# Constants built on VectorE instead of with iotas on GpSimd, and keys and values of a batch projected side by side in 512 columns

## The chip, the cores and the metric

One core of one Trainium2 chip. The metric is the device time of one execution in microseconds (us), median of several executions. A profile of one execution goes with each kernel; its span is about 2 us shorter than the execution's time. Times inside a profile are counted from the start of its span. "Granted clock" is the share of TensorE's full clock that an execution was given, by its record. TensorE, VectorE (DVE), ScalarE (ACT), GpSimd (POOL) and SyncE (SP) are the engines; PEld is TensorE's loading of weights.

## The reference

Attention with projected keys and values, then a gated feed-forward. Cut to what matters:

```python
# q, k, v: 8 batches, 8 heads, 1024 rows, 64 wide; E, F: 64 x 1024
k_proj = np.einsum('ks,bhsd->bhkd', E, k)
v_proj = np.einsum('ks,bhsd->bhkd', F, v)
scores = (1 / 8) * np.matmul(q, k_proj.transpose(0, 1, 3, 2))   # 1024 x 64 a head
attn = exp(scores - max) / (sum + 1e-09)
x = np.matmul(attn, v_proj)                       # heads put side by side: 8192 x 512
out = (sigmoid(x @ w_gate) * (x @ w_val)) @ w_out # 512 -> 1536 -> 512
```

All inputs and the output are float32; the kernel casts to bf16 on loading.

## The kernel before: the parts that matter

The kernel records operations with what they read and write; a wait is made of each dependence. The loads of k, q, v and the weights cast, and are all issued by GpSimd, in this order. E and F come through SyncE.

```python
load_k(0)
pool(lambda e: e.iota(col_i[:, :], [[1, P]], channel_multiplier=0), w=["col_i"])
pool(lambda e: e.iota(row_i[:, :], [[1, 1]], channel_multiplier=1), w=["row_i"])
load_q_half(0, 0)
load_v(0)
# ... three more iotas for patterns ...
load_w(0)          # w_gate and w_val, first piece (256 of 1536 columns)
load_w(1)
load_q_half(0, 1)
load_w(2)
load_w(3)
```

VectorE makes an identity of the counted columns and rows, and selectors for the softmax's sums:

```python
dve(lambda e: e.tensor_copy(col_f[:, :], col_i[:, :]), ["col_i"], ["col_f"])
dve(lambda e: e.tensor_copy(row_f[:, :], row_i[:, :]), ["row_i"], ["row_f"])
for t, n in ((identf, "identf"), (ident, "ident")):
    dve(lambda e, t=t: e.tensor_scalar(t[:, :], col_f[:, :], row_f[:, 0:1], None, op0=ALU.is_equal), ...)
# ... half, low_i, low_f, negm, dsel8, bsel8, bsel, dsel ...
```

TensorE begins with the first half batch. It cannot do a thing before the identity:

```python
start_loads()
constants()
project_consts()          # E and F turned with identf: 8 transposes, then EFT on ScalarE
busy(56)                  # 56 dummy 128x128 matmuls, to warm the clock
bk = whole.next()
project(0, 0, [bk, bk], 0)    # k, needs EFT and the k load
keep_k(bk, 0)
turn_k(whole)
qt, sc, den, bc, xo = half_unit(0, whole)
qt(0); qt(1)              # q transposes, need the first q half
sc(0); sc(1)              # scores and exp
den()                     # sums, reciprocal
bks = [whole.next(), whole.next()]
project(1, 1, bks, 0)     # v, needs the v load
keep_v(bks, 0, ["ACT", "DVE", "ACT", "DVE"])
busy(8); bc(0); busy(4); xo(0); bc(1); xo(1); busy(10)
# then the feed-forward of batch b, with the attention of batch b+1 in between
```

From the third batch on (six batches), keys and values are projected together in the middle of the feed-forward, in 32 matmuls of 256 columns, and the keys are turned by a DMA transpose:

```python
def kv():
    bk = att.next()
    project(2 * b % 3, 0, [bk, bk], 0)           # keys: 16 matmuls of 256 columns
    project((2 * b + 1) % 3, 1, [bk, bk], 256)   # values: 16 more
    # ... b == 1 differs ...
    act(kpd[:, :, :, :], bank[bk][:, 0:256] ... .to_broadcast([P, NR, 2, DH]), ...)  # 128 x 512
    keep_v([bk, bk], 256, ["ACT"] * 4)           # four copies, 64 x 256 each
```

The softmax here doesn't subtract the row's maximum and nothing guards it: scores larger than these inputs give would overflow.

Of the kernel before, what the change touches and what calls it, by code (L numbers as in the profile page):

```python
# [7 lines left out]
ALU = mybir.AluOpType  # L8
# [110 lines left out]
def bass_linformer_attn__then__ffn_glu_sigmoid_kernel(  # L119
# [18 lines left out]
    with contextlib.ExitStack() as es:  # L138
# [5 lines left out]
        col_i = sbuf("col_i", [P, P], I32)  # L144
        row_i = sbuf("row_i", [P, 1], I32)
        pat_i = sbuf("pat_i", [P, P], I32)
        pat4_i = sbuf("pat4_i", [P, 64], I32)
        eight_i = sbuf("eight_i", [P, 8], I32)
        low_i = sbuf("low_i", [P, 3], I32)
        col_f = sbuf("col_f", [P, P], FP32)  # L150
        row_f = sbuf("row_f", [P, 1], FP32)
        pat_f = sbuf("pat_f", [P, P], FP32)
        pat4_f = sbuf("pat4_f", [P, 64], FP32)
        eight_f = sbuf("eight_f", [P, 8], FP32)
        low_f = sbuf("low_f", [P, 2], FP32)
        half = sbuf("half", [P, 2], FP32)
        negm = sbuf("negm", [P, 1], FP32)
# [13 lines left out]
        kpd = sbuf("kpd", [P, NR, 2, DH], BF16)  # L171
# [114 lines left out]
        def start_loads():  # L286
            for src, rows, n in ((E, slice(0, 64), "E"), (F, slice(64, 128), "F")):
                add(
                    "SP",
                    lambda e, src=src, rows=rows: e.dma_start(EF[rows, :], src[:, :]),  # L290
                    w=[("EF", n)],
                    dma="in" + n,
                )
            load_k(0)
            pool(lambda e: e.iota(col_i[:, :], [[1, P]], channel_multiplier=0), w=["col_i"])
            pool(lambda e: e.iota(row_i[:, :], [[1, 1]], channel_multiplier=1), w=["row_i"])
            load_q_half(0, 0)
            load_v(0)
            pool(
                lambda e: e.iota(  # L300
                    pat_i[:, :], [[-2, 4], [0, 4], [1, 8]], channel_multiplier=0
                ),
                w=["pat_i"],
            )
            pool(lambda e: e.iota(eight_i[:, :], [[1, 8]], channel_multiplier=0), w=["eight_i"])
            pool(
                lambda e: e.iota(
                    pat4_i[:, :], [[-2, 2], [0, 8], [1, 4]], channel_multiplier=0
                ),
                w=["pat4_i"],  # L310
            )
            load_w(0)
            load_w(1)
            load_q_half(0, 1)
            load_w(2)
            load_w(3)

        def constants():
            dve(lambda e: e.tensor_copy(col_f[:, :], col_i[:, :]), ["col_i"], ["col_f"])
            dve(lambda e: e.tensor_copy(row_f[:, :], row_i[:, :]), ["row_i"], ["row_f"])  # L320
            for t, n in ((identf, "identf"), (ident, "ident")):
                dve(
                    lambda e, t=t: e.tensor_scalar(  # L323
                        t[:, :], col_f[:, :], row_f[:, 0:1], None, op0=ALU.is_equal
                    ),
                    ["col_f", "row_f"],
                    [n],
                )
            for n, op in ((0, ALU.is_ge), (1, ALU.is_lt)):
                dve(  # L330
                    lambda e, n=n, op=op: e.tensor_scalar(  # L331
                        half[:, n : n + 1], row_f[:, :], 64.0, None, op0=op
                    ),
                    ["row_f"],
                    [("half", n)],
                )
            for n, bit in ((0, 7), (1, 8), (2, 3)):
                dve(
                    lambda e, n=n, bit=bit: e.tensor_single_scalar(
                        low_i[:, n : n + 1], row_i[:, :], bit, op=ALU.bitwise_and  # L340
                    ),
                    ["row_i"],
                    [("low", n)],
                )
            for n in range(2):
                dve(
                    lambda e, n=n: e.tensor_copy(low_f[:, n : n + 1], low_i[:, 2 * n : 2 * n + 1]),
                    [("low", 2 * n)],
                    [("low_f", n)],
                )  # L350
            dve(
                lambda e: e.tensor_scalar(negm[:, :], low_i[:, 1:2], -0.125, None, op0=ALU.mult),
                [("low", 1)],
                ["negm"],
            )
            dve(lambda e: e.tensor_copy(pat_f[:, :], pat_i[:, :]), ["pat_i"], ["pat_f"])
            dve(lambda e: e.tensor_copy(eight_f[:, :], eight_i[:, :]), ["eight_i"], ["eight_f"])
            for n in range(2):
                dve(
                    lambda e, n=n: e.tensor_scalar(  # L360
                        dsel8[:, n, :, :].rearrange("p a c -> p (a c)"),
                        pat_f[:, :],
                        half[:, n : n + 1],
                        None,
                        op0=ALU.is_equal,
                    ),
                    ["pat_f", ("half", n)],
                    [("dsel8", n)],
                )
            dve(  # L370
                lambda e: e.tensor_scalar(
                    bsel8[:, :, :, :].rearrange("p c h d -> p (c h) d"),
                    eight_f[:, :].unsqueeze(2).to_broadcast([P, 8, 64]),
                    low_f[:, 0:1],
                    0.5,
                    op0=ALU.is_equal,
                    op1=ALU.mult,
                ),
                ["eight_f", ("low_f", 0)],
                ["bsel8"],  # L380
            )
            dve(
                lambda e: e.tensor_scalar(
                    bsel[:, :, :, :].rearrange("p c h d -> p (c h) d"),
                    eight_f[:, 0:4].unsqueeze(2).to_broadcast([P, 4, 64]),
                    low_f[:, 1:2],
                    0.25,
                    op0=ALU.is_equal,
                    op1=ALU.mult,
                ),  # L390
                ["eight_f", ("low_f", 1)],
                ["bsel"],
            )
            dve(lambda e: e.tensor_copy(pat4_f[:, :], pat4_i[:, :]), ["pat4_i"], ["pat4_f"])
            for n in range(2):
                dve(
                    lambda e, n=n: e.tensor_scalar(
                        dsel[:, n, :, :].rearrange("p a c -> p (a c)"),
                        pat4_f[:, :],
                        half[:, n : n + 1],  # L400
                        None,
                        op0=ALU.is_equal,
                    ),
                    ["pat4_f", ("half", n)],
                    [("dsel", n)],
                )
# [79 lines left out]
        def half_unit(hf, ring):  # L486
# [51 lines left out]
            def den():  # L538
                bk = ring.next()
                for n in range(4):  # L540
                    for c in range(4):
# [21 lines left out]
                        rhl[:, 0:P], rhi[:, 0:P], negm[:, 0:1], rden[:, 0:P], ALU.mult, ALU.add  # L563
                    ),
                    [("rden", 0), "rhi", "negm"],
# [67 lines left out]
        def attention(b):  # L633
            s = b % 2

            def kv():
                bk = att.next()
                project(2 * b % 3, 0, [bk, bk], 0)
                project((2 * b + 1) % 3, 1, [bk, bk], 256)
                if b == 1:  # L640
                    keep_k(bk, 0)
                    keep_v([bk, bk], 256, ["ACT"] * 4)
                    return
                act(
                    kpd[:, :, :, :],
                    bank[bk][:, 0:256]
                    .rearrange("p (r d) -> p r d", r=NR)
                    .unsqueeze(2)
                    .to_broadcast([P, NR, 2, DH]),
                    [],  # L650
                    ["kpd"],
                    b=bk,
                )
                keep_v([bk, bk], 256, ["ACT"] * 4)

            def turn_kd():
                if b == 1:
# [5 lines left out]
                        kpD[:, :, :].rearrange("p (r h) c -> p r (h c)", h=2),  # L663
                        kpd[:, :, :, :].rearrange("p r g d -> p (r g d)"),
# [56 lines left out]
            def split():  # L721
                rd = [("rden", c) for c in range(4)]
                dve(lambda e: e.tensor_copy(rhi[:, :], rden[:, :]), rd, ["rhi"])  # L723
                dve(
                    lambda e: e.scalar_tensor_tensor(  # L725
                        rhl[:, :], rhi[:, :], negm[:, 0:1], rden[:, :], ALU.mult, ALU.add
                    ),
                    rd + ["rhi", "negm"],
                    ["rhl"],
                )  # L730
# [189 lines left out]
        load(wO[:, :, :], moe_w_out.rearrange("(m p) c -> p m c", p=P), ["wO"], "wO")  # L920

# [85 lines left out]
```

## Time and profile before

| | before |
|---|---|
| time, median of 4 executions | 580.79 us |
| span of the profile | 577.98 us |
| TensorE's first matmul | 15.48 |
| projection of k, of v (first half batch) | 21.21, 27.59 |
| first feed-forward matmul at full pace | 33.46 |
| from there to the end | 544.5 |
| one projection of keys and values, third batch on, in the chain | 1.87 |

The last column of a timeline line, in brackets, is how long the engine had been idle before it and what ended that. A line of the chain gives its start, its length, and what was at work. The lines themselves are in the prediction below.

### The profile page before, as it was taken

What the parts mean: (1) busy time and instruction counts of PE and PEld (TensorE: products, weight loads), DVE (VectorE), ACT (ScalarE), POOL (GpSimd) and SP (SyncE); (2) the same over time, 40 slices, a digit from 0 to 9 for tenths busy, and PEclk for the clock granted to TensorE, in tenths of its full rate; (3) what the DMA queues carried; (4) which work ended last, traced back from release to release, by engine and by line L of the source; (5) the groups of instructions that cost most, each with busy time, mean ns of one, the idle gap of its engine ahead of it and who ended that gap; (6) DMA issues with size and microseconds to landing.
All of it is one profiled execution on the core that took longest, in us unless ns stands there. A gap on an engine that the chain in (4) does not pass through costs nothing.

```text
span 578.0 us, 7834 instructions
## 1 busy us (share of the span) xinstructions
PE 555.5 (96%) x3110; PEld 252.1 (44%) x3110; DVE 246.4 (43%) x381; ACT 175.1 (30%) x317; POOL 101.5 (18%) x139
## 2 busy tenths in 40 slices
PE   0899999999999999999999999999999999999997
PEld 0644434544444444444444444444445444444443
DVE  0446355335443356235363354433562353633332
ACT  0355443352223422333223522234223332222220
POOL 1800010102600053000810026000520008000000
PEclk9999999999999999999999999999999999999999
DMA  6999979892576047650696125771311011100002
GB/s 109 160 203 200 186 125 194 150 195 58 108 148 119 37 65 134 127 90 36 111 173 104 44 57 108 148 119 37 75 56 45 21 38 38 37 36 19 36 37 91
DMA packets 74212, 56.01 MB, mean 97 GB/s; under 512 B 34528, under 2 KB 65760, under 8 KB 74176
## 3 DMA queue, kind: packets, MB, share of 16 engines
q0 software_dynamic: 31776, 29.89, 33.7%
q1 hardware_dynamic: 42400, 25.63, 17.5%
q8 instruction: 24, 0.39, 0.3%
q14 instruction: 12, 0.10, 0.1%
HBM read 60.29 MB, written 16.78 MB: 133 GB/s over the span
## 4 chain that ended last, share of the span: by engine, by line
PE 94%; issue 2%; DVE 2%; ACT 1%; POOL 0%; POOLq 0%; DVEq 0%
PE pF L218 85%; PE pA L218 9%; DVE rden L715 1%; ACT eT L222 0%; DVE xT L606 0%; ACT qT L222 0%; POOL KV L236 0%; DVE rden L553 0%; DVE vpD L464 0%; DVE identf L323 0%; DVE rhl L725 0%; DVE ost L878 0%; DVE hT L851 0%; DVE rhi L723 0%; ACT kp L222 0%
## 5 line engine op out<-in xcount | busy, mean ns | idle before, releaser
L851 DVE SCALAR_TENSOR_TENSOR hT<-sig,pF 128x512 bf16<-128x512 f32 x192 | 130.9, 685 | 203.3 <-PE pF L218 155.8
L222 ACT ACTIVATE sig<-pF 128x512 f32<-128x512 f32 x192 | 114.8, 599 | 315.9 <-PE pF L218 312.9
L218 PE MATMUL pF<-xT,wG 128*128 128x512 bf16 x768 | 198.6, 380 | 0.6 <-ACT rb L222 0.3
L218 PE MATMUL pF<-xT,wV 128*128 128x512 bf16 x768 | 198.2, 379 | 0.2 <-DVE xT L606 0.2
L218 PE MATMUL pF<-wO,hT 128*128 128x512 bf16 x720 | 165.4, 380 | 0.0
L218 PEld LDWEIGHTS pF<-xT,wV 128*128 128x128 bf16 x768 | 75.1, 98 | 90.9 <-issue 0.6
L218 PEld LDWEIGHTS pF<-xT,wG 128*128 128x128 bf16 x768 | 72.1, 98 | 94.2 <-issue 11.8
L760 POOL PARTITION_BROADCAST rb<-rrow x96 | 70.8, 798 | 219.3 <-DMA rrow<-rden 213.9
L218 PEld LDWEIGHTS pF<-wO,hT 128*128 128x128 bf16 x720 | 69.1, 98 | 87.3 <-issue 5.8
L878 DVE TENSOR_SCALAR ost<-pF 128x512 f32<-128x512 f32 x60 | 41.5, 691 | 94.0 <-PE pF L218 94.0
L222 ACT ACTIVATE eT<-pA 128x512 bf16<-128x512 f32 x63 | 32.7, 603 | 10.2 <-PE pA L218 10.2
L785 DVE TENSOR_TENSOR xT<-pA,rb 128x512 bf16<-128x512 f32 x56 | 34.7, 681 | 0.0
L715 DVE RECIPROCAL rden<-pA 128x128 f32<-128x128 f32 x28 | 23.7, 909 | 0.0
L236 POOL DMA_DIRECT2D KV<-in_k_dram x8 | 7.5, 937 | 82.4 <-PE pF L218 80.4
L236 POOL DMA_DIRECT2D KV<-in_v_dram x8 | 7.2, 895 | 75.0 <-PE pA L218 75.0
L218 PE MATMUL pA<-identf,EF 128*128 128x128 f32 x8 | 1.9, 421 | 15.5 <-DVE half L331 15.5
L218 PE MATMUL pA<-KV,EFT 128*64 128x256 bf16 x240 | 14.6, 274 | 0.0
L218 PEld LDWEIGHTS pA<-KV,EFT 128*64 128x64 bf16 x240 | 12.5, 110 | 3.1 <-issue 3.0
L222 ACT ACTIVATE kpd<-pA 128x512 bf16<-128x512 f32 x6 | 3.6, 597 | 28.4 <-PE pA L218 28.4
L218 PE MATMUL pA<-eT,vpD 64*64 64x512 bf16 (+1 forms) x136 | 10.4, 370 | 0.3 <-DVE vpD L464 0.3
L218 PE MATMUL pA<-qT,kpD 64*64 64x512 bf16 (+1 forms) x140 | 10.4, 367 | 0.3 <-ACT qT L222 0.3
L222 ACT ACTIVATE vpD<-pA 64x256 bf16<-64x256 f32 x28 | 10.5, 375 | 0.5
(74 smaller groups left out, 109.1 us busy)
## 6 DMA issues: line engine op xcount, KB each, us to landing
out_dram<-ost SPq DMA_DIRECT2D x64, 256.0 KB, 2.0
KV<-in_k_dram POOLq DMA_DIRECT2D x8, 1024.0 KB, 10.7
KV<-in_v_dram POOLq DMA_DIRECT2D x8, 1024.0 KB, 11.3
Qb<-in_q_dram POOLq DMA_DIRECT2D x7, 1024.0 KB, 15.2
wO<-in_moe_w_out_dram POOLq DMA_DIRECT2D x1, 1536.0 KB, 44.5
Qb<-in_q_dram POOLq DMA_DIRECT2D x2, 512.0 KB, 10.3
wG<-in_moe_w_gate_dram POOLq DMA_DIRECT2D x2, 512.0 KB, 18.3
wV<-in_moe_w_val_dram POOLq DMA_DIRECT2D x2, 512.0 KB, 20.1
```

Source lines behind the costliest of these rows:

```text
L218: return add("PE", lambda e: e.matmul(o, lhsT, rhs, **kw), r=r, x=[("bank", b)])
L222: return add("ACT", lambda e: e.activation(o, i, func, scale=scale), r=r, w=w, x=x)
L236: add("POOL", lambda e: e.dma_start(o, i), r=r, w=w, dma=sem)
L715: lambda e, cc=cc: e.reciprocal(rden[:, cc], bank[bk][:, cc]),
L760: lambda e, n=n, i=2 * rnd + c, j=j, parts=parts: e.partition_broadcast(rb[0:parts, n, :], rrow[32 * j : 32 * j + 1, i, :], channels=parts),
L785: lambda e, r=r, g=g, n=n, bk=bks[g]: e.tensor_tensor(xT[s][:, r, :, 256 * g : 256 * g + 256], bank[bk][:, :].rearrange("p (f c) -> p f c" ...
L851: lambda e: e.scalar_tensor_tensor(hT[blk % 2][:, m, :], sg[:, :], 1.0, bank[pv][:, :], ALU.add, ALU.mult,),
L878: lambda e: e.tensor_scalar(o[:, :], bank[pb][:, :], 0.5, None, op0=ALU.mult),
```

## The change

Its intent: no iota, so that GpSimd needs no library of code before the loads of q and v and before the identity; and half as many matmuls in the six later projections. The row and column counters are made on VectorE by doubling a counted row, and a 32x32-block transpose of it; GpSimd only writes 0, 32, 64 and 96 into the four quarters of a column. The library for the broadcasts (first needed for the third batch) is loaded by an instruction of its own after the first batches' loads.

```diff
+            for i in range(4):
+                pool(lambda e, i=i: e.memset(quad[32 * i : 32 * i + 32, :], 32.0 * i), w=[("quad", i)])
             load_k(0)
-            pool(lambda e: e.iota(col_i[:, :], [[1, P]], channel_multiplier=0), w=["col_i"])
-            pool(lambda e: e.iota(row_i[:, :], [[1, 1]], channel_multiplier=1), w=["row_i"])
             load_q_half(0, 0)
             load_v(0)
-            (three more iotas)
...
+            dve(lambda e: e.memset(count[:, 0:1], 0.0), [], ["count"])
+            for i in range(7):
+                n = 1 << i
+                dve(... e.tensor_scalar(count[:, n : 2 * n], count[:, 0:n], float(n), None, op0=ALU.add) ...)
+            (four patterns, one transpose, row_f = rows + quad)
...                                   # the identity and the selectors from these
+                for t in range(NT):
+                    for w in range(2):            # keys, then values, of step t
+                        n = (2 * b + w) % 3
+                        src = KV[n][:, :, :].rearrange("p h (t d) -> p t h d", t=NT)
+                        mm(bk, bank[bk][64 * w : 64 * w + 64, :], EFT[:, t, 64 * w : 64 * w + 64],
+                           src[:, t, :, :], ..., tp=(0, 64 * w))       # 512 columns
-                act(kpd ...)                      # 128 x 512
-                keep_v([bk, bk], 256, ["ACT"] * 4)
+                act(kpd ...)                      # 64 x 1024
+                for g in range(2):
+                    act(vpD[64 * g : 64 * g + 64, :, :] ..., bank[bk][64:128, :], ...)   # 64 x 512
...
-                        kpD[:, :, :].rearrange("p (r h) c -> p r (h c)", h=2),
-                        kpd[:, :, :, :].rearrange("p r g d -> p (r g d)"),
+                        kpD[:, :, :],
+                        kpd[:, :, :, :].rearrange("p h g d -> p (h g d)"),
...
+        pool(lambda e: e.load_library(spread_library))    # after the load of w_out
```

## The prediction

> **What bounds the kernel now.** I read the page's busy shares and the chain that ended last first, then the timeline of the first 35 us, then the DMA view, then the chain again around one projection. All times below are us from the span's start unless said otherwise.
>
> ```profile
> PE 555.5 (96%) x3110; PEld 252.1 (44%) x3110; DVE 246.4 (43%) x381; ACT 175.1 (30%) x317; POOL 101.5 (18%) x139
> ...
> PE   0899999999999999999999999999999999999997
> ...
> PE 94%; issue 2%; DVE 2%; ACT 1%; POOL 0%; POOLq 0%; DVEq 0%
> ```
>
> TensorE is busy in every slice but the first, and 94% of the chain is its own work. Whatever moves no TensorE time and no start of TensorE is worth nothing. The first slice is empty, and the timeline says why:
>
> ```profile
> 1.24 1.01 POOL L236 DMA_DIRECT2D KV<-in_k_dram  x1 [0.80 <-POOLq L992]
> 1.38 0.57 SPq L290 DMA_DIRECT2D EF<-in_F_dram  x1
> 13.96 0.23 POOL L295 IOTA col_i<- 128x128 int32 x1 [11.71 <-issue]
> ...
> 14.24 1.07 POOL L236 DMA_DIRECT2D Qb<-in_q_dram  x1
> 14.55 0.78 DVE L323 TENSOR_SCALAR identf<-col_f,row_f 128x128 f32<-128x128 f32 x1
> 15.48 1.94 PE L218 MATMUL pA<-identf,EF 128*128 128x128 f32 x8 [15.48 <-DVE half L331]
> 17.22 4.07 PE L218 MATMUL pF<-ident 128*128 128x128 bf16 x56
> 21.21 1.06 PE L218 MATMUL pA<-KV,EFT 128*64 128x256 bf16 x16
> 27.59 1.06 PE L218 MATMUL pF<-KV,EFT 128*64 128x256 bf16 x16
> ```
>
> GpSimd sits 11.71 before the first iota, behind a library load that the instruction order shows there and the trace gives no busy time. Everything hangs on it: the identity for TensorE (first matmul at 15.48), and, because GpSimd issues in order, the loads of q and v at 14.24 and 15.33. The DMA view of the first 20 us gives the landings:
>
> ```profile
> KV<-in_k_dram POOLq DMA_DIRECT2D x1, 1024.0 KB, 11.1
> KV<-in_v_dram POOLq DMA_DIRECT2D x1, 1024.0 KB, 10.6
> ...
> EF<-in_F_dram SPq DMA_DIRECT2D x1, 256.0 KB, 4.2
> ```
>
> So k lands at 1.24+11.1=12.3, F at 1.38+4.2=5.6, v at 15.33+10.6=25.9. The DMA engines stand idle from about 12.3 to 16.
>
> The chain around one of the six steady projections, which the second part of the change rewrites:
>
> ```profile
> 160.55 12.19 PE pF L218 x56
> 172.74 1.87 PE pA L218 x32
> 174.61 13.06 PE pF L218 x60
> 187.66 0.56 PE pA L218 x8
> ```
>
> **What the Trainium skill says.** "GPSIMD Engine Reference", section 2.1 Instruction dispatch: the first call to a freshly loaded kernel pays about 6 us for fetching it, with no visible profile instruction. The trace agrees that nothing is visible, but the gap is 11.71, and I use that. "TensorEngine Tiling (Array Packing)", section Tiling Modes and its Key Properties: with 128 rows and 64 columns there are two tiles, and different tiles run in parallel. The trace agrees: 32 projection matmuls of 273 ns each take 1.87, not 8.7. They already run in pairs, 117 ns a pair of 256 columns. "DMA: Bandwidth & Descriptors", section Queues, rings and completion order: an engine takes turns between queues, a packet at a time. The trace agrees: the transpose of the keys lands in 2.4 in the last batch, with no loads in flight, and 9.4 in the median.
>
> **The change, part 1: constants.** Removed: five iotas and their library load on GpSimd. Added: four memsets ahead of the k load (memsets at the span's start follow each other by 0.03, so the k load goes out about 0.2 later), and a chain on VectorE: one memset, seven adds, each waiting for the last, four pattern copies, one 128x128 transpose, one add, then the identity. The small VectorE instructions at 14.23 to 15.8 follow each other by 0.1 to 0.2; estimate: 13 by 0.15, plus 0.4 for the transpose and 0.5 for the identity, is 2.9, from about 0.8, so done near 3.7. F lands at 5.6. So the identity is no longer the last to arrive; E and F are. TensorE starts near 5.6 instead of 15.48, almost 10 sooner. This is not the gain, since the next thing it needs is data.
>
> Follow TensorE in the new order. Transposes of E and F 5.6 to 7.5 (1.94). The 56 warming matmuls, 3.9 by the chain, to 11.4. Keys: the load lands at 12.3+0.2=12.5; TensorE waits 1.1. The k projection and what follows to the q transposes took 21.28 to 23.19 in the chain, 1.9: so 14.4. The q half now queues directly behind k instead of 2 us after an idle queue. Rate: between v's landing (25.9) and the landing of the next batch's q (issued 23.72, 26.3 to landing: 50.0) 4608 KB landed in 24.1, that is 191 KB per us, the queue full. So the q half (512 KB) lands 2.7 after k, at 15.2, and v (1024 KB) 5.4 later, at 20.6. The q transposes start at 15.2 (before 23.1); from there to the v projection took 4.4 (23.19 to 27.59), so TensorE is ready at 19.6 and waits for v until 20.6. Before, v had landed at 25.9 and was used at 27.59. So the v projection moves by 27.6-20.6=7.0. The rest, to the first full feed-forward matmuls at 33.46, is arithmetic: the denominator's reciprocal is now done while v is awaited, which takes the two VectorE copies of v (0.44 each) forward, but the warming matmuls (0.6 and 0.4) and the copies of rb on ScalarE stay in the way; I give 0.3 for it. Gain of part 1: about 7.2.
>
> Is it kept? The DMA queue gains only 25.9-20.6=5.3, so each later load has up to 1.9 less slack. Slack before, from issue plus landing in the trace: second piece of w (needed 36.8, landed 31 to 32) 5; third w_val piece (needed 42.5, landed 39.9) 2.6; next v (issued 25.46, landed 36.6 later, at 62.1, needed 65.9) 3.8; w_out (landed 26.33+44.5=70.8, needed 74.8) 4.0. All stay above zero, the smallest at 0.7. The library for the broadcasts is now loaded by an own instruction after the last of these loads, when GpSimd has nothing to do until about 69 (it idles 48 there before), and its first broadcast comes at 140. Hidden.
>
> **Part 2: the projection in 512 columns.** Before, 16 pairs of 256 columns; after, 8 pairs of 512. Columns streamed are the same. The full matmuls follow each other by 13.06/60=218 ns for 512 columns, and 109 for 256 would be half of it, so 16 by 109 is 1.74 of the 1.87 and the rest, 0.13, is the change of tile shape at the ends, which stays. Nothing but a few ns per instruction is saved: 0.03 to 0.1 a batch, six batches, 0.3. On ScalarE: one 128x512 copy of 0.60 becomes a 64x1024 one (a 1024-wide copy of q takes 1.02), four 64x256 of 0.38 become two of 64x512 of about 0.60: 2.1 before, 2.2 after. ScalarE is 30% busy and TensorE did not wait for it there (60 matmuls in 13.06 are at full pace). Worth 0.
>
> The keys' transpose is issued 0.4 later (longer copy). It moves the same 128 KB, as 8 blocks of 64x128 instead of 4 of 128x128. Before, issued at 175.36, it landed 9.6 later, at 184.9; the scores need it at 187.66. Slack 2.7, after the change about 2.3 if it is as fast. No wait.
>
> **Sum.** 581.4 - 7.2 - 0.3 = 573.9.
>
> **The rivals.** (a) The whole early start is gained: TensorE starts 9.9 sooner and k, q, v come in time. For it: part of k's slow transfer (47 to 140 GB/s between 4.2 and 6.3, against 200 near 10) could be the library load itself, and with it gone k, q and v would all land up to 2 sooner. Against: that stretch is also the very first traffic. It would give 571.5 or so. (b) The loads share instead of queueing: with q, v and weights behind it, k lands later, 14 rather than 12.5, and the gain shrinks to 5 or less: 576. Against it: successive landings on this queue come one by one in issue order. (c) The transposed keys arrive late: if blocks of 64 rows cost more packets, 9.6 becomes 13 or more with loads in flight, and TensorE waits 1 to 5 in five of six batches: 575 to 595. For it: little slack, 2.7. Against: the trace shows it as 512 packets of 256 bytes, one row of 128 elements each, and the new blocks have as many such rows. (d) TensorE, now idle in short pieces while it awaits k, q and v, loses granted clock; the clock row shows nine tenths throughout, with similar gaps at 24 to 31. 1 to 3 lost.
>
> **Range and chances.** The center is 573.9. (a) and (b) give plus or minus 2.5; (c) and (d), with some 15% together, lengthen the upper side. Range 571.0 to 577.5. Faster by over 2% needs 569.8, that is 11.6 gained: more than the 9.9 by which TensorE's start can move at all plus 0.3, so 3%. Slower by over 2% needs (c) at its worst: 3%. Within 2%: 94%.
>
> **What would show it.** First TensorE matmul at 5.5 to 6, released by the loads of E and F; k projection near 12.5 and v projection near 20.6, each after an idle stretch on TensorE that ends with a DMA; feed-forward from 26 instead of 33.5; then the same chain, with 1.8 to 1.87 per projection and no wait at the scores. It is wrong if the identity is ready only after 6, if k lands outside 11.5 to 14, if a weight piece or v makes TensorE wait after 26, or if the scores wait for the transposed keys.

## The result, and the profile after

572.9 us, median of 4 executions (572.26 to 574.05), against 580.79 for the kernel before, median of 4 executions too. The ratio is 0.9866, with a 95% interval of 0.9843 to 0.9889; it is the mean time of one kernel's fast executions over that of the other's in the same rounds, so not quite the ratio of the two medians. The result is correct. The prediction, 573.9 with a range of 571.0 to 577.5, holds.

The timeline of the changed kernel's start, TensorE's lines with two of GpSimd and one of VectorE:

```profile
1.34 1.02 POOL L228 DMA_DIRECT2D KV<-in_k_dram  x1
...
2.36 0.88 POOL L228 DMA_DIRECT2D Qb<-in_q_dram  x1
...
3.90 0.29 DVE L348 TENSOR_SCALAR identf<-count,row_f 128x128 f32<-128x128 f32 x1
...
5.57 1.94 PE L210 MATMUL pA<-identf,EF 128*128 128x128 f32 x8 [5.57 <-DMA EF<-in_F_dram]
...
7.31 5.20 PE L210 MATMUL pF<-ident 128*128 128x128 bf16 x56
...
12.44 1.06 PE L210 MATMUL pA<-KV,EFT 128*64 128x256 bf16 x16
...
14.95 1.07 PE L210 MATMUL pF<-ident,Qb 128*128 128x128 bf16 x16 [0.53 <-DMA Qb<-in_q_dram]
...
20.74 1.06 PE L210 MATMUL pF<-KV,EFT 128*64 128x256 bf16 x16 [1.25 <-DMA KV<-in_v_dram]
...
26.06 0.39 PE L210 MATMUL pF<-xT,wG 128*128 128x512 bf16 x1
```

The identity is ready at 4.2, and the first matmul waits for F. From there on TensorE's waits end with loads: 0.53 for the q half, 1.25 for v. The feed-forward starts at 26.06, 7.40 sooner than before, where the same line is

```profile
33.46 0.39 PE L218 MATMUL pF<-xT,wG 128*128 128x512 bf16 x1
```

The chain around one of the later projections:

```profile
165.32 1.85 PE pA L210 x16
167.16 2.26 PE pF L210 x10
169.43 0.05 issue
169.48 10.74 PE pF L210 x49
180.22 0.56 PE pA L210 x8
```

16 matmuls take 1.85 where 32 took 1.87. From the start of the projection to the scores it is 14.90 (180.22-165.32), before 14.92 (187.66-172.74). The piece of issue in between is no wait: this trace lacks 54 of 3014 matmul records (2960 matmuls against 3014 weight loads), and a missing one leaves a hole. From the feed-forward's start to the end of the span it is 544.40 now and was 544.53 before. So 7.40 of the 7.53 that the span lost lie in the first 34 us, and the six projections give the other 0.13. These are single executions: both profiled ones were among the quicker of their kernel (579.88 against a median of 580.79, 572.26 against 572.90), and by the medians the gain is 7.89.

### The profile page after: what moved, and what is told of

The parts are those of the page before. It is cut to its first block, busy times and chain, and to the rows that moved or that the text cites. A ratio compares the mean times of both kernels' runs of the same rounds, so it can differ in the third digit from the quotient of the medians.

```text
span 570.5 us, 7585 instructions
## 1 busy us (share of the span) xinstructions
PE 552.1 (97%) x2960; PEld 248.6 (44%) x3014; DVE 247.8 (43%) x392; ACT 175.7 (31%) x305; POOL 100.4 (18%) x138
## 4 chain that ended last, share of the span: by engine, by line
PE 85%; DMA 10%; POOL 2%; DVE 1%; issue 1%; SPq 0%; ACT 0%; DVEq 0%; POOLq 0%
PE pF L210 78%; PE pA L210 7%; DMA Qb<-in_q_dram 6%; DMA qT<-Qb 4%; DVE rden L719 1%; POOL wG L228 1%; POOL wV L228 1%; POOL KV L228 0%; POOL Qb L228 0%; SPq L607 0%; DVE rhl L729 0%; DVE ost L882 0%; DVE hT L855 0%; ACT sig L214 0%; DVE rhi L727 0%
## 5 line engine op out<-in xcount | busy, mean ns | idle before, releaser
L210 PE MATMUL pF<-xT,wG 128*128 128x512 bf16 x747 | 194.5, 379 | 2.3 <-issue 1.4
L210 PE MATMUL pF<-wO,hT 128*128 128x512 bf16 x702 | 163.5, 379 | 1.5 <-issue 0.8
L214 ACT ACTIVATE eT<-pA 128x512 bf16<-128x512 f32 x63 | 32.7, 603 | 10.2 <-PE pA L210 10.2
L214 ACT ACTIVATE kpd<-pA 64x1024 bf16<-64x1024 f32 x6 | 6.1, 1017 | 28.3 <-PE pA L210 28.3
L210 PE MATMUL pA<-KV,EFT 128*64 128x512 bf16 (+1 forms) x144 | 14.5, 346 | 0.0
L210 PE MATMUL pA<-wO,hT 128*128 128x512 bf16 x47 | 10.5, 379 | 0.1
L210 PEld LDWEIGHTS pA<-KV,EFT 128*64 128x64 bf16 x144 | 7.4, 109 | 6.8 <-issue 3.0
L214 ACT ACTIVATE rb<-pA 128x512 f32<-128x512 f32 x14 | 7.5, 617 | 4.9 <-PE pA L210 4.9
```

The source lines that it names most:

```text
L210: return add("PE", lambda e: e.matmul(o, lhsT, rhs, **kw), r=r, x=[("bank", b)])
L214: return add("ACT", lambda e: e.activation(o, i, func, scale=scale), r=r, w=w, x=x)
```

## The experiments

All runs gave right results and ran in the fast state, or as a single look (e6, e7) in an unknown one. Spans and times inside are of the profiled execution; the time is the median of all. "Feed-forward" is the second weight load of w_gate, which no trace lacks.

| run | k proj. | v proj. | feed-forward | span | time | ratio to before, 95% interval |
|---|---|---|---|---|---|---|
| before | 21.21 | 27.59 | 33.46 | 577.98 | 580.79 | |
| changed | 12.44 | 20.74 | 26.05 | 570.46 | 572.90 | 0.9866, 0.9843 to 0.9889 |
| e1, constants alone | 12.63 | 20.38 | 25.69 | 570.95 | 572.78 | 0.9866, 0.9853 to 0.9879 |
| e2, projection alone | 22.05 | 28.43 | 34.29 | 578.70 | 580.68 | 1.0003, 0.9990 to 1.0016 |
| e3, iotas ahead of k | 18.95 | 27.11 | 32.98 | 577.50 | 580.50 | 0.9995, 0.9981 to 1.0008 |
| e4, loads ahead of iotas | 24.27 | 30.65 | 36.52 | 581.04 | 582.61 | 1.0032, 1.0018 to 1.0045 |
| e5, early identity, late loads | 12.20 | 24.63 | 31.46 | 575.86 | 577.56 | 0.9938, 0.9925 to 0.9952 |
| e6, 76 warming matmuls | 13.14 | 21.69 | 28.89 | 574.43 | 576.23 | one look |
| e7, 40 warming matmuls | 12.25 | 20.00 | 25.31 | 569.71 | 571.54 | one look |
| e8, v in halves | 12.51 | 19.95 | 24.66 | 569.28 | 572.20 | 0.9854, 0.9839 to 0.9869 |
| e9, waits filled | 12.25 | 20.61 | 25.92 | 570.56 | 572.45 | 0.9852, 0.9838 to 0.9867 |
| e10, halves and filled | 12.58 | 20.39 | 25.11 | 569.79 | 571.59 | 0.9842, 0.9828 to 0.9856 |
| e11, changed again | 12.45 | 20.66 | 25.97 | 570.77 | 573.34 | 0.9866, 0.9846 to 0.9886 |

e1 to e4 shared one chip and 11 executions of the kernel before (580.65), e5 to e8 another and 9 (581.03), e9 to e11 again 9 (581.06).

### e1: the new constants with the old projection

```diff
 (the changed kernel, but)
-    (16 matmuls of 512 columns, kpd 64 x 1024, two copies of values)
+    (32 matmuls of 256 columns, kpd 128 x 512, four copies, as before)
```

> Part 1 alone (new constants, old projection). Theory: the early start is nearly the whole gain; the chain of the changed kernel shows 1.85 us per projection instead of 1.87, six times, so this kernel should be only 0.1 to 0.2 us slower than the changed one: span 570.6 to 570.8 us, ratio to the kernel before 0.9865 to 0.9875, and the projection in the chain 1.87 us. Rival: the wider projection brings a microsecond or more of the gain; then the span here is 571.5 us or more.

The ratio is that of the whole change, 0.9866. The profiled span, 570.95, is a little above the 570.6 to 570.8 that was expected, though its feed-forward starts at 25.69, sooner than in the changed kernel. The projection is 1.87 in its chain, so the wider projection does not explain that. It was lost later, at a wait that the prediction had not listed: the scores of the second batch wait for its transposed queries. The timeline of TensorE near 70 us in this run:

```profile
71.17 0.41 PE L210 MATMUL pA<-qT,kpD 64*64 64x512 bf16 x4 [1.07 <-DMA qT<-Qb]
...
78.82 0.40 PE L210 MATMUL pA<-rhl,bsel 32*128 32x512 bf16 x4 [0.43 <-DVE rhl L708]
```

and at the same place in the kernel before:

```profile
77.45 0.63 PE L218 MATMUL pA<-qT,kpD 64*64 64x512 bf16 x8
...
85.84 0.40 PE L218 MATMUL pA<-rhl,bsel 32*128 32x512 bf16 x4 [0.95 <-DVE rhl L725]
```

TensorE waits 1.07 for the queries (with the pieces around it, the feed-forward goes on 1.26 later than it would have: 1.82 after the scores began, before 0.56), and gets 0.52 back because it then waits less for the reciprocal (0.43 instead of 0.95). From the feed-forward's start to the end this execution took 545.26, 0.73 more than the kernel before.

### e2: the new projection with the old constants

```diff
 (the kernel before, but)
-    (32 matmuls of 256 columns, kpd 128 x 512, four copies)
+    (16 matmuls of 512 columns, kpd 64 x 1024, two copies of values)
```

> Part 2 alone (new projection, old constants). Theory: 0.02 us per projection, so span 577.8 to 578.0 us and ratio 0.9995 to 1.000; ScalarE's wider key copy (1.02 instead of 0.60 us) delays the transposes' issue by 0.4 us, they land within 8.5 to 10 us of their issue with loads in flight, as before, and the scores never wait. Rival 1: 0.3 to 1 us is saved (span 577.0 to 577.7). Rival 2: the transposes of 64-row blocks land later than 12 us and the scores wait: span 580 us or more.

Ratio 1.0003: nothing that shows in the time. The span of the profiled execution came out 0.72 above that of the kernel before, outside what was expected; its start was later (feed-forward 34.29 against 33.46, with the same code there), which is the spread of the start. From the feed-forward to the end it took 544.40, 0.13 less than before (544.53), and the same as in the changed kernel. That is 0.02 for each of six projections. The keys' transpose, by the view of its tile in this run:

```profile
L222 ACT ACTIVATE kpd<-pA x6: 1017/1017/1017, 108.1 to 445.2; 64x1024 bf16<-64x1024 f32 x6
...
DMA to landing us min/median/max: 2.6/7.6/9.3
```

ScalarE's copy takes 1.02, as predicted. Blocks of 64 rows land in a median of 7.6 and at most 9.3; before it was 9.4 and 9.6. No wait at the scores follows.

### e3: the first two iotas ahead of the k load

```diff
+            (the iotas of col_i and row_i)
             load_k(0)
-            (the iotas of col_i and row_i)
```

> The kernel before, with the first two iotas put ahead of the k load, so that the library load has no transfer of GpSimd's in flight. It asks what the 11.7 us gap is made of. Theory A: the library load takes 11.6 us by itself: first iota at about 12.8, k issued at 13.2, landed at 24.3, v landed at 32.4 instead of 25.9 and used then: slower by about 4.8 us, 585.6. Theory B: the load is short (about 6 us, as the Trainium skill has it) and in the kernel before it waited for the k load in flight (landed at 12.35): first iota at about 7, k landed at 18.6, v at 26.7: 580 us, about the same.

The timeline, GpSimd's first iota and TensorE:

```profile
8.30 0.23 POOL L294 IOTA col_i<- 128x128 int32 x1 [7.87 <-issue]
...
18.95 1.06 PE L218 MATMUL pA<-KV,EFT 128*64 128x256 bf16 x16 [2.63 <-DMA KV<-in_k_dram]
```

With no transfer of GpSimd's in flight the first iota comes at 8.30. GpSimd is free at about 1.24 (when it issued k in the kernel before), so the library load takes some 7.1 (7.6 if it begins at 0.72, where the changed kernel's first memset stands), not 11.6. Theory A falls. (Theory B's 6 us are those of "GPSIMD Engine Reference", section 2.1, which the prediction names.) k is issued later and lands later; the time is the same as before, 580.5, as theory B had it. k took 10.3 from issue to landing here, with the library already loaded, against 11.1 in the kernel before: most of k's slow transfer is not the library load's doing. TensorE, which had nothing to do for 2.63 before k landed, then ran at half clock from 21.3 to 28.2; the granted clock was 0.991 to 0.994 in all four executions of this kernel.

### e4: the loads of q and v ahead of the iotas

```diff
             load_k(0)
-            (the iotas of col_i and row_i)
             load_q_half(0, 0)
             load_v(0)
+            (the iotas of col_i and row_i)
```

> The kernel before, with the loads of the first q half and of v put ahead of the first two iotas: the data comes early, the identity does not. Common to both theories: no gain, since TensorE starts with the identity. Theory A (library load 11.6 us by itself, from 4.1): first iota at 15.7, first matmul at 17.3, v projection at 29.4 instead of 27.6: 582.6 us. Theory B (the library load waits for the transfers in flight, q half and v landing near 20.6): first iota at 21 to 22.5, first matmul near 23.5, v projection near 35.5: 588 to 589.5 us. If instead early data were the whole cause of the gain, this would be faster than the kernel before by 5 us.

```profile
16.70 0.23 POOL L297 IOTA col_i<- 128x128 int32 x1 [12.69 <-issue]
...
17.91 1.94 PE L218 MATMUL pA<-identf,EF 128*128 128x128 f32 x8 [17.91 <-DVE identf L323]
...
30.65 1.07 PE L218 MATMUL pF<-KV,EFT 128*64 128x256 bf16 x16
```

The library load took 12.69 and ended at 16.70, while v landed only at 20.8 in the trace: it does not wait for the transfers in flight, so theory B falls as well in its strict form. What the two runs leave is that the load takes 7.1 with none of GpSimd's loads in flight, 11.7 with k in flight (12.2 in e2, whose start has the same code), and 12.7 with k, q and v: it takes longer with transfers in flight. That q and v add to what k does is not shown, since 12.7 is as far from 12.2 as 12.2 is from 11.7. How transfers lengthen it, the runs do not show. With the data early and the identity late, the kernel is 2.0 us slower than before by the medians. That this is the 582.6 of theory A is luck: its load of 11.6 by itself had fallen with e3, and its v projection at 29.4 came at 30.65. (The v projection is 3.06 later than in the profile of the kernel before, which was a quick execution.)

### e5: the early identity with late loads

```diff
 (the changed kernel, but)
-            load_q_half(0, 0)
+            load_q_half(0, 0, r=[("KV", 0)])     # issued when k has landed
```

> The changed kernel, with one wait added: the first q half's load is issued only when k has landed, so v and all that follow stand behind it too. The identity stays early, the loads become late. Theory (the start is set by v's landing): the q half lands at about 12.3+5.8=18.1 us, v at about 24, so the v projection moves from 20.74 to 24.0 and the feed-forward from 26.06 by 3.3: span about 573.8 us, 43% of the gain gone. Rival (the early identity is what counts, the loads have slack): span stays within 0.5 us of 570.5.

```profile
17.75 1.83 PE L210 MATMUL pF<-ident,Qb 128*128 128x128 bf16 x16 [3.58 <-DMA Qb<-in_q_dram]
...
24.63 1.92 PE L210 MATMUL pF<-KV,EFT 128*64 128x256 bf16 x16 [1.37 <-DMA KV<-in_v_dram]
```

v is projected at 24.63, near the 24.0 of the theory, and TensorE waits for it. The rival falls: the loads had no slack. But the feed-forward starts at 31.46, not 29.3, and the span is 2.1 above what was expected: 0.6 because v is later than 24.0, and 1.5 between v's projection and the feed-forward (6.83, in the changed kernel 5.31). The views of these stretches show it (columns: stretch, length, busy time and count on TensorE, weight loads, VectorE, ScalarE, GpSimd, then granted clock, DMA share, GB/s):

```profile
14.44:17.86 3.42, 0.10 (x2) 0.11 (x3) 0.00 (x0) 0.44 (x1) 3.42 (x6) 1.00 1.30 170
...
17.86:28.10 10.24, 8.40 (x82) 5.71 (x82) 3.08 (x6) 3.75 (x8) 6.33 (x8) 0.50 1.32 192
```

After 3.4 us in which TensorE did almost nothing, it ran at half clock for 10.2 us. The v projection takes 1.92 instead of 1.06.

e1, e4 and e5 together with the two kernels make a square:

| | loads late | loads early |
|---|---|---|
| identity late | before | e4: +2.0 us |
| identity early | e5: -3.5 us | changed, e1: -7.9 us |

(e4, e5 and e1 are the differences of the medians.) Neither half brings the gain alone. e5's cell is not the late loads alone: about 1.5 of what it lost went to the half clock, as estimated from the two stretches above.

### e6 and e7: more and fewer warming matmuls

```diff
-        busy(56)
+        busy(76)      # e6
+        busy(40)      # e7
```

> The changed kernel with 76 warming matmuls instead of 56: 1.1 us more of work on TensorE ahead of the k projection, without an idle stretch. Theory (v's landing sets the start, TensorE waited 1.25 us for it): k projection at 13.5 instead of 12.44, v projection still within 0.2 us of 20.74, feed-forward within 0.2 of 26.06, span 570.3 to 570.8 us. Rival (TensorE's own chain sets it): everything 0.6 to 1.1 us later, span 571.1 to 571.6 us.

> The changed kernel with 40 warming matmuls instead of 56: TensorE is done with them near 11.5 and waits about 0.8 us for k. Theory (data sets the start): no gain, v projection within 0.2 us of 20.74. Rival: 0.2 us sooner or more, since the k projection can follow k's landing (12.3) at once. A third outcome, seen in the run with the iotas first, is that the idle stretch costs granted clock: then the clock row shows a stretch at half, and the span grows by 0.5 us or more.

e6 came out 3 to 4 us longer than either theory had it, and is no clean answer. Its k projection comes at 13.14, and its v projection, in the timeline, at 21.69:

```profile
21.69 1.92 PE L210 MATMUL pF<-KV,EFT 128*64 128x256 bf16 x16 [1.57 <-DMA KV<-in_v_dram]
```

The view of a stretch of the same run, with the columns as above:

```profile
20.67:30.91 10.24, 9.00 (x76) 5.38 (x78) 4.36 (x9) 2.93 (x6) 0.00 (x0) 0.50 1.38 201
```

TensorE still waited for v (1.57), so more work ahead of it cost nothing there. v itself landed 0.9 later in this execution (at 21.64, against 20.70), and the clock fell to half from 20.67 on. Both can happen to the changed kernel too, so one look cannot lay them to the extra matmuls. e7 is the other way round: the k projection follows k's landing at once (12.25, after a wait of 1.84), v landed at 19.95, the clock held, and the span is 0.8 shorter. By its number the rival came out, but the wait for v is there again (0.50), so the 0.8 is v's earlier landing, not the shorter warming. In all traces of the changed kernel and its variants that have v in one piece (e1, e5, e6, e7, e9, e11), the v projection starts within 0.1 us of v's landing, or up to 0.6 after it where dummy matmuls were put in between (e9). v's landing is what sets the start, and it varies.

### e8: v in halves

```diff
-            load_v(0)
+            for R in range(2):
+                load(KV[1][:, 4 * R : 4 * R + 4, :], (v of batch 0, heads 4 * R to 4 * R + 3), ...)
...
-        project(1, 1, bks, 0)
-        keep_v(bks, 0, ["ACT", "DVE", "ACT", "DVE"])
-        busy(8); bc(0); busy(4); xo(0); bc(1); xo(1); busy(10)
+        for R in range(2):      # a half's 16 matmuls of 128 columns, and its copies
+            bks = [whole.next(), whole.next()]
+            project_v_half(bks, R)
+            keep_v_half(bks, R, (["ACT"] * 4, ["DVE"] * 4)[R])
+        bc(0); bc(1); xo(0); xo(1); busy(16)
```

(also the four memsets behind the k load)

> An attempt to beat the changed kernel, from what the runs showed: v of the first batch is loaded and projected in two halves of four heads, so that the first half (landing about 2.7 us before the second) is projected while the second is still on its way; the warming matmuls in the middle of the start are dropped; the four memsets go behind the k load. Theory: the last v copies end near 22, the normalisations follow at once, the feed-forward starts at 24.8 instead of 26.06: span about 569.3 us, ratio to the kernel before 0.984 to 0.986. Rival 1: ScalarE's copies (four of v, four of rb) become the limit and the gain is under 0.4 us. Rival 2: gained at the start, lost later, at a load (the third piece of w_val lands at 33.8 and is needed near 34) or at the transposed queries of the second batch (landing at 70.5, needed near 69): span 570 us or more.

The feed-forward starts at 24.66 and the span is 569.28, as expected. Over five executions the time is 572.2 (571.22 to 573.41), ratio 0.9854: the saving is there in the profiled execution, but the others are up to 2 us longer. That is not the clock: the profiled execution, the quickest of the five, is the only one with a lower clock (0.997), and the others have 1.0. What made them longer is not shown.

### e9, e10 and e11: filling the waits

Why does the clock fall, in e3, e5, e6 and e8? It was below 0.998 in 2 of 4 executions of the changed kernel, and in none of those of the kernel before. e9 puts dummy matmuls where TensorE waits for q and v. e10 does the like in e8. e11 is the changed kernel again, on the same chip.

```diff
 (e9: the changed kernel, but)
         turn_k(whole)
+        busy(8)
...
         den()
+        busy(20)
 (e10: e8, with busy(8) after turn_k, busy(4) ahead of each part of den, busy(4) ahead of bc(0))
```

> The changed kernel with 28 more dummy matmuls, 8 where TensorE waits for the first q half and 20 where it waits for v (0.06 us each at full clock, so 0.5 and 1.1 us, about as long as the waits of 0.53 and 1.25). It asks why the granted clock fell to half for 3.4 to 10.2 us near the start in 2 of 4 executions of the changed kernel, and in none of the 20 of the kernel before. Theory (TensorE's idle stretches while it waits for data cost it the clock): all executions here at clock 1.0, span 570.3 to 571.2 us in each. Rival (the clock falls for a reason that idleness has nothing to do with): lower clocks in about half of the executions again.

> The version with v in halves, and TensorE's waits filled with dummy matmuls (8 before the q transposes, 4 before each part of the denominator, 4 before the broadcast). Theory: first halves' saving of 1.2 us stays and the half-clock stretch at 16.9 us of the run without fillers goes: span 568.8 to 569.8 us, time 571.0 us, ratio to the kernel before 0.983 to 0.985, all executions at clock 1.0. Rival: the spread of 571 to 573 us that it showed comes from v's landing (19.95 to 21.6 us in the runs so far), not from the clock: clock 1.0 throughout and the same spread.

> The changed kernel itself once more, on the same chip as the two others, for their comparison and for how often its clock falls. Expected: 572.3 to 574.1 us, ratio 0.985 to 0.988, and a granted clock below 1.0 in 1 to 4 of 6 executions, if waiting for data is the cause.

| | executions: span, granted clock |
|---|---|
| changed, first round | 570.5, 1.0; 571.1, 1.0; 572.2, 0.994; 571.1, 0.994 |
| e11, changed again | 570.8, 1.0; 570.2, 0.999; 572.5, 0.996; 572.3, 0.997 |
| e9 | 570.6, 570.8, 571.3, 570.0: all 1.0 |
| e10 | 569.8, 570.2, 569.8, 569.8, 570.5: all 1.0 |
| before | 29 executions, all 1.0 |

(0.999 is a half clock in the last microsecond, after TensorE's work: e7 has it, from 568.5 on.) 4 of 8 executions of the changed kernel fall below 0.998 (with e1, 6 of 12), and 0 of 9 with fillers. By these counts, and by e3 and e5, where long waits had it fall in all eight executions, TensorE's waits for data are the likely cause of the lost clock. They do not decide it alone: e7 waited 1.84 for k and kept the clock, and e8, which has no fillers either, lost it in 1 of 5. The four have a mean span of 572.0, the other four 570.65. The 1.4 between them need not all be the clock's: a late v makes the wait longer and the end later by itself, as in e6, and only the profiled executions show when v landed. In e1 the same difference is 0.45, and in e8 the execution with the lower clock is the quickest. e11's times, 571.95 to 574.27, reach a little beyond what was expected at both ends. e9's spans keep within 570.0 to 571.3, also a little wider than expected, though its dummy matmuls ended 0.6 after v had landed (20.61 against 20.01), so they cost a little too. e10 is the best version by its median: 571.59 us, five executions within 0.7, ratio 0.9842. It beats the kernel before by 1.6%, and the changed kernel of the same call by 1.75 us by the medians (571.59 against 573.34), though the intervals of the two ratios overlap (0.9828 to 0.9856 and 0.9846 to 0.9886). The span of its profiled execution, 569.8, lies at the upper edge of what was expected, and the time 0.6 above; TensorE waits 0.40 for the transposed queries of the second batch in it. The rival for e10, that v's landing would keep up the same spread, falls for these five executions. But since e8's longer executions had the full clock, a kept clock does not explain why e10 spreads less; that stays open.

## Why the prediction was right, point by point

- **The identity.** Predicted near 3.7 and hidden behind F at 5.6. It was ready at 4.2 (the seven adds took 0.24 each, not 0.15), F released TensorE at 5.57. Right, and the square shows that it is necessary: e4 has the data early without it, and gains nothing.
- **The next limits are loads.** k at 12.5, the q half at 15.2, v at 20.6 were predicted; the uses were at 12.44, 14.95 and 20.74. Estimating a full queue's rate from a later stretch of the same trace (191 KB per us) carried this. Right, and e5 shows it: with the loads late again, 3.5 of the 7.9 remain (about 5 without the half clock, by the estimate above).
- **The warming matmuls.** Predicted to end at 11.4, with a wait of 1.1 for k. They took 5.20 instead of 4.07 and ended at 12.51: the full clock came only at 11.3 in this execution, 5.7 after the first matmul (3.4 in the kernel before); up to there the matmuls follow each other by 106 ns, after it by 56. So the step was wrong, but hidden: k landed at 12.27.
- **Part 2.** Predicted 0.3, measured 0.13 (e2 and the changed kernel alike). The few ns per instruction that were to be saved are 1.2 (0.02 over 16 fewer instructions). The term was more than twice too large, and too small to matter.
- **The keys' transpose.** No wait, as predicted. It landed even sooner than before, 7.6 against 9.4 in the median, with blocks of 64 rows. Rival (c) falls.
- **The slack of later loads.** All loads on the list came in time, with less slack, as predicted: the least is again the third piece of w_val (landed 33.83, used at 35.04, so 1.2; before 2.6). The list lacked one transfer: the transposed queries of the second batch, needed 2.2 after they landed before (75.3 against 77.5), and with TensorE 7.4 sooner not in time. In the changed kernel, TensorE's timeline has it as a longer group of scores (0.96 instead of 0.63), and the shorter wait for the reciprocal (0.62 instead of 0.95) gives it back:

```profile
70.05 0.96 PE L210 MATMUL pA<-qT,kpD 64*64 64x512 bf16 x8
...
78.44 0.39 PE L210 MATMUL pA<-rhl,bsel 32*128 32x512 bf16 x4 [0.62 <-DVE rhl L729]
```

This changes the chain that ended last. In the kernel before it is almost all TensorE's work from 33.46 on; in the changed kernel it reaches these scores through the load of the second batch's queries and their transposes, and not through v. So a still earlier start is lost in part here: e10 waits 0.40 at this place, and takes 544.68 from the feed-forward's start to the end, against 544.40. The chain of the changed kernel:

```profile
10.85 33.15 DMA Qb<-in_q_dram
44.01 11.87 DMA qT<-Qb
...
67.42 3.05 DMA qT<-Qb
...
70.60 0.41 PE pA L210 x4
```

- **Rival (a)**, that the library load had slowed k and all data would come much sooner: k took 11.1 from issue to landing before, 10.9 after (1.34 to 12.27), 10.3 in e3. With no library load beside it, it took 10.3 to 11.5 in all runs, with it 11.1 to 11.9 (before, e2, e4). So at most a small part of it, no clear step above the spread. **Rival (b)**, that the loads behind k delay it: k landed at 12.27, no later than before. It falls. **Rival (d)**, a lost clock: it was given a small chance, and it happens in half of the changed kernel's executions, which are 1.4 us longer in the mean; how much of that is the clock's and how much a late v's is not shown. With the waits filled (e9) it did not happen in 4 executions.

That the time lies a microsecond below the center has a plain part: the kernel before measured 580.79 in the rounds of the result, not the 581.4 that the prediction started from. And the sum came out better than its terms, which is luck: v's projection moved by 6.85, not 7.0, the rest of the start gave 0.55, not 0.3, the projections 0.13, not 0.3, and together they make 7.53 in the profiles against 7.5. (7.0 and 0.3 are 7.3; the prediction writes 7.2.) v's landing alone differs by 1.7 us between executions, so that it fell on 20.70, with 20.6 predicted, is in part luck too.

## What to carry to other kernels

An engine that issues loads in order should do nothing ahead of them that fetches code: what it delays is all data behind it. When such a delay goes, do the sum again with what then comes last: here nearly 10 us sooner for TensorE became 7.4, since v's landing took over. And look at every transfer that the moved engine will meet sooner, to the second batch and beyond, and at what the engine does while it waits, since long idle stretches may cost it clock (e3 and e5).

## What the Trainium skill lacked or had wrong

- "GPSIMD Engine Reference", section 2.1 Instruction dispatch, gives about 6 us for the first call to freshly loaded code. Here the load took 7.1 with none of GpSimd's loads in flight (e3), 11.7 and 12.2 with the k load in flight (before, e2), 12.7 with k, q and v in flight (e4). The page does not say that it takes longer with transfers in flight. That the profile shows no instruction for it agrees.
- "TensorE: Matmul & The Clock Gate", Part 1, table of the two states, has half clock after an idle window of about 3.4 us. Half clock lasted 3.4, 6.8 or 10.2 us in e8, e3, e5 and e6, whole multiples of 3.41, which agrees with its window. But the clock fell after stretches in which TensorE was far from idle: the 3.4 us ahead of the fall in e6 have 2.23 us of busy matmuls and 1.03 of weight loads, in e8 1.74 and 1.32. In the changed kernel a stretch with 1.97 and 1.43 was kept at full clock, in e7 one with 1.71 and 1.54 (8.69 to 12.11). What decides stays open. The same page, under "A second HAM failure mode", does tell of a clock that falls through short idle pieces, without saying how much idleness it takes.
- No page that I read has a figure for how far apart a load's sixteen completion counts can lie when loads follow each other. v's came between 17.8 and 20.7 in the changed kernel, and between 25.3 and 25.9 in the kernel before, where the queue had run empty ahead of q. v's landing varied from 19.95 to 21.64 between executions that had v in one piece behind k and q. Which of the sixteen is late, and why, these runs do not show.
